# Two requests for key rows move from SyncE to ScalarE's queue, and steps of the engines are put in another order

## The chip, the cores and the metric

The kernel runs on one core of one Trainium2 chip. The metric is device time in microseconds, as the median of several executions; lower is better. The core has TensorE (PE in the profile), VectorE (DVE), ScalarE (ACT), GpSimd (POOL) and SyncE (SP), each with an instruction stream of its own that it works through in order, and 16 DMA engines that carry out transfers which an engine's instruction asks for.

## The reference

Attention in chunks of 64 tokens, then a feed-forward layer with a short convolution as its gate. Shapes: q, k, v are 8 x 8 x 576 x 64, so d_model = 512 and d_ff = 1024.

```
scores = scale * matmul(q_c, k_c.T)          # per head, chunk of 64
attn = exp(scores - max); attn = attn / (sum(attn) + 1e-09)
x = matmul(attn, v_c)  -> (batch, seq, heads * head_dim)
h = maximum(x @ w_in, 0)
conv_out = sum over k of conv_w[k] * shifted h
out = (h * sigmoid(conv_out)) @ w_out
```

The weights arrive as 64-bit floats and are turned into pairs of 32-bit ones on the chip.

## The kernel before, in words

The work is cut into 36 attention tiles of 128 tokens (two chunks each), and into 12 units of 384 tokens for the first product of the feed-forward layer (x @ w_in, line 411, called MM1 here). The second product (line 515) takes tokens by pairs of tiles. x and the weights are kept as a high and a low part (x_h and x_l, wi_h and wi_l), so that each product takes three passes.

For an early tile, rows of q and k are loaded into one of three buffers (`load_rows`, line 129; the buffers are named qk with a number), transposed on TensorE (line 198) in two halves, and each half is copied out of PSUM into qkT by ScalarE or VectorE (lines 77 and 79). Then come the scores (line 250), the maximum, the subtraction, the exponential, the sum and the scaling (lines 260 to 282 and 322), a transposition of the result (line 329), the product with v (line 342), and x_h and x_l (lines 397 and 401). The weights are loaded into two buffers (line 547; w_in in six pieces, conv_w, then w_out) and split by lines 561, 565, 570, 77 or 79, and 574. MM1 of the first unit needs tiles 0 to 2.

Nothing is scheduled while the kernel runs. A list `steps` holds every step. A table `moved_` says which steps go to another engine than their usual one, a table `order_` gives the order in which a planner places them, and the planner's begin times give the order in which each engine gets its instructions. Loads and stores are all issued by SyncE, in order, and the issue of a load waits until its buffer is free. Each transfer signals one of eight semaphores in turn, so an issue also waits until the transfer eight places before it has landed.

Two pieces of code are written out around the steps. The constants: `ident_r`, a copy of the identity that ScalarE makes, and `rebias`. And filler matmuls (line 1161), products of `ident_r` with itself whose result nobody reads. They are put on TensorE where the planner sees a gap, up to its planned time 110, and the first group stands at the very start. Their number follows from the length of the gap.

Of the kernel before, what the change touches and what calls it, by code (L numbers as in the profile page):

```python
# [23 lines left out]
AF = mybir.ActivationFunctionType  # L24
# [6 lines left out]
def attn_ffn(ctx: ExitStack, tc: tile.TileContext, q, k, v, w_in, conv_w, w_out, out):  # L31
    nc = tc.nc
# [5 lines left out]
    NCK = S // C  # L38
# [33 lines left out]
    steps = []  # L72
# [20 lines left out]
    ident = const.tile([P, P], F32, name="ident")  # L93
    make_identity(nc, ident)
    ident_r = const.tile([P, P], F32R, name="ident_r")
    nc.scalar.copy(out=ident_r, in_=ident)
    rebias = const.tile([P, 1], F32, name="rebias")
    nc.scalar.activation(out=rebias, in_=ident[:, 0:1], func=AF.Exp)
    nc.gpsimd.memset(rebias, -896.0 * 2 ** 23)
# [23 lines left out]
    def load_rows(st, t):  # L123
        if t < NP:
            r = row_slot(st).rearrange("(p two) (h c) -> two p h c", two=2, h=H)
            (b0, t0), (b1, t1) = chunk(2 * t), chunk(2 * t + 1)
            for i, src in enumerate((q, k)):
                for b, t_, p0, n in [(b0, t0, 0, C)] if b0 == b1 else [(b0, t0, 0, C // 2), (b1, t1, C // 2, C // 2)]:
                    nc.sync.dma_start(out=r[i, p0:p0 + n], in_=src[b, :, t_:t_ + 2 * n, :].rearrange("h (p e) d -> p h (e d)", e=2))  # L129
            return  # L130
        r = row_slot(st).rearrange("p (i c) -> p i c", i=2)
        (b0, t0), (b1, t1) = chunk(2 * t), chunk(2 * t + 1)
        for i, src in enumerate((q, k)):
            rows = r[:, i].rearrange("p (h d) -> p h d", d=D)
            for b, t_, p0, n in [(b0, t0, 0, P)] if b0 == b1 else [(b0, t0, 0, C), (b1, t1, C, C)]:
                nc.sync.dma_start(out=rows[p0:p0 + n], in_=src[b, :, t_:t_ + n, :].rearrange("h i d -> i h d"))
# [557 lines left out]
    def att(t, key, load_key, writes):  # L694

        st = {"t": t}
        if t < NAT:
            r = "slot"
            ld = step("SP", 1.25 if (2 * t) % NCK < NCK - 1 else 2.5, load_key, load_rows, (st, t), take=[(r, st)],
# [259 lines left out]
    for s, over in x_writes:  # L959
# [21 lines left out]
    ]  # L981
    for i, n in (divmod(x, 4) for x in moved_):
# [171 lines left out]
    for i in sorted(order_, key=lambda i: begin[i]):  # L1154
# [11 lines left out]
        steps[i]["fn"](*steps[i]["args"], *([steps[i]["eng"]] if steps[i]["other"] else []))  # L1166
        if steps[i]["port"]:
            made[i] = list(nc.cur_bb.bb.instructions)[n:]
# [40 lines left out]
```

## Time and profile before

| | us |
|---|---|
| median of 3 executions | 469.8 (469.11 to 470.95) |
| the profiled execution, its own time | 470.28 |
| its span, first to last instruction | 468.5 |
| PE busy in the span | 456.2 (97%) |
| DVE busy | 409.6 (87%) |
| ACT busy | 263.7 (56%) |
| POOL busy | 283.5 (61%) |

Matmuls are pipelined and overlap in the records, so a busy PE is an engine that always has something under way. The profiled execution took 1.78 us more than its span, and 0.48 us more than the median.

### The profile page before, as it was taken

To read this page: it belongs to the slowest core of one execution; us is meant where nothing else is said; L and a number is where in the kernel's file an instruction comes from. 1 tells how busy PE (TensorE), PEld (TensorE's weight loads), DVE (VectorE), ACT (ScalarE), POOL (GpSimd) and SP (SyncE) were. 2 spreads that over 40 slices of the span, in tenths; PEclk is the share of its full clock that TensorE was granted. 3 is DMA by queue.
4 is the path that set the end of the run, shared out by engine and by line. 5 is a ranking of instruction groups with operands and counts; after the bars stand their busy time and mean duration, and the time that the engine had idled before them with its cause. 6 is when DMAs were issued, how large, how long until landed. Compare 5 with 4: busy or idle time off the path is not lost.

```text
span 468.5 us, 13076 instructions
## 1 busy us (share of the span) xinstructions
PE 456.2 (97%) x5287; PEld 444.3 (95%) x5287; DVE 409.6 (87%) x771; ACT 263.7 (56%) x544; POOL 283.5 (61%) x256
## 2 busy tenths in 40 slices
PE   7899899999999999999999999999999999999996
PEld 7779798999999999999999999999999999999996
DVE  2899999999999899989788889998989987977784
ACT  3589988756646555564444564455556453542641
POOL 0344768847686654979678967755856643448221
PEclk9999999999999999999999999999999999999999
DMA  7999999999896839687987495741215101100012
GB/s 223 248 305 306 246 149 218 158 177 209 147 158 175 191 95 178 126 158 180 181 182 182 109 172 111 169 128 33 58 35 157 25 24 29 40 17 31 22 46 91
DMA packets 184320, 64.32 MB, mean 137 GB/s; under 512 B 155564, under 2 KB 175044, under 8 KB 184260
## 3 DMA queue, kind: packets, MB, share of 16 engines
q1 hardware_dynamic: 184260, 63.48, 62.7%
q8 instruction: 42, 0.69, 0.6%
q14 instruction: 18, 0.15, 0.1%
HBM read 50.88 MB, written 23.59 MB: 159 GB/s over the span
## 4 chain that ended last, share of the span: by engine, by line
PE 80%; DVE 9%; DMA 5%; ACT 2%; issue 1%; SPq 1%; POOL 1%; DVEq 0%; ACTq 0%; POOLq 0%
PE b_ps L411 36%; PE b_ps L515 36%; DVE gt L454 2%; PE sx_ps L250 2%; PE sx_ps L342 2%; PE z_ps L342 2%; DMA v<-in_v 1%; DMA w<-in_moe_w_out 1%; DVE f L502 1%; DMA qk<-in_k 1%; DMA w<-in_moe_conv_w 1%; DVE wt L570 1%; PE z_ps L250 1%; PE b_ps L329 1%; SPq L129 1%
## 5 line engine op out<-in xcount | busy, mean ns | idle before, releaser
L515 PE MATMUL b_ps<-wo_h,f 128*128 128x256 f32 x1008 | 190.9, 282 | 0.4 <-DVE wt L533 0.3
L515 PEld LDWEIGHTS b_ps<-wo_h,f 128*128 128x128 f32 x1008 | 158.8, 188 | 2.0 <-issue 0.5
L515 PE MATMUL b_ps<-wo_l,f 128*128 128x256 f32 x504 | 141.2, 280 | 0.0
L454 DVE SCALAR_TENSOR_TENSOR gt<-b_ps,cw,gt 128x384 f32<-128x384 f32 (+3 forms) x208 | 116.4, 576 | 11.2 <-ACT gt L449 9.1
L502 POOL TENSOR_TENSOR f<-gt,f 128x512 fp32r<-128x512 f32 x67 | 86.4, 1294 | 45.5 <-ACT f L77 16.3
L515 PEld LDWEIGHTS b_ps<-wo_l,f 128*128 128x128 f32 x504 | 94.9, 188 | 0.0
L411 PE MATMUL b_ps<-x_h,wi_h 128*128 128x386 f32 (+2 forms) x384 | 84.6, 342 | 0.0
L411 PE MATMUL b_ps<-x_l,wi_h 128*128 128x386 f32 (+2 forms) x384 | 83.3, 339 | 0.0
L411 PE MATMUL b_ps<-x_h,wi_l 128*128 128x386 f32 (+2 forms) x384 | 83.1, 338 | 0.0
L465 ACT ACTIVATE gt<-gt 128x384 f32<-128x384 f32 (+2 forms) x96 | 49.9, 524 | 54.5 <-DVE gt L454 54.2
L411 PEld LDWEIGHTS b_ps<-x_l,wi_h 128*128 128x128 f32 x384 | 68.8, 188 | 0.0
L411 PEld LDWEIGHTS b_ps<-x_h,wi_l 128*128 128x128 f32 x384 | 68.6, 188 | 0.0
L449 ACT ACTIVATE gt<-b_ps,cw 128x384 f32<-128x384 f32 (+2 forms) x104 | 56.5, 556 | 20.6 <-DVE b_ps L421 18.5
L411 PEld LDWEIGHTS b_ps<-x_h,wi_h 128*128 128x128 f32 x384 | 65.5, 188 | 1.0 <-ACT gt L449 0.2
L505 POOL TENSOR_TENSOR gt<-gt 128x512 f32<-128x512 f32 x41 | 52.8, 1295 | 15.3 <-DVE gb L505 6.0
L484 DVE SCALAR_TENSOR_TENSOR gt<-gt,b_ps 128x192 f32<-128x192 f32 (+2 forms) x120 | 47.2, 410 | 8.8 <-ACT gt L465 8.5
L419 ACT ACTIVATE b_ps<-b_ps 128x386 f32<-128x386 f32 (+2 forms) x79 | 37.6, 479 | 28.2 <-PE b_ps L411 27.0
L79 POOL CAST f<-gt 128x512 fp32r<-128x512 f32 x43 | 26.9, 625 | 21.2 <-PE b_ps L515 18.0
L527 ACT ACTIVATE wt<-b_ps 128x256 f32<-128x256 f32 x54 | 20.6, 381 | 29.8 <-PE b_ps L515 29.7
L77 ACT CAST f<-gt 128x512 fp32r<-128x512 f32 x44 | 26.9, 617 | 14.8 <-PE b_ps L515 8.5
L502 POOL TENSOR_TENSOR f<-gb,f 128x512 fp32r<-128x512 f32 x18 | 23.2, 1294 | 17.9 <-DVE f L502 9.9
L220 DVE STREAM_TRANSPOSE qkT<-qk 128x1024 f32<-128x1024 f32 (+1 forms) x30 | 33.4, 1121 | 0.0
(99 smaller groups left out, 585.6 us busy)
## 6 DMA issues: line engine op xcount, KB each, us to landing
out<-wt SPq DMA_DIRECT2D x36, 256.0 KB, 2.7
qk<-rows SPq DMA_DIRECT2D x24, 320.0 KB, 5.8
rows<-in_q SPq DMA_DIRECT2D x12, 576.0 KB, 8.1
rows<-in_k SPq DMA_DIRECT2D x12, 576.0 KB, 7.8
qk<-rows SPq DMA_DIRECT2D x24, 256.0 KB, 4.6
v<-in_v SPq DMA_DIRECT2D x21, 256.0 KB, 5.0
w<-in_moe_w_out SPq DMA_DIRECT2D x4, 1024.0 KB, 6.5
wt<-wt SPq DMA_DIRECT2D x48, 64.0 KB, 2.0
```

The costliest lines, as they stand in the source:

```text
L77: nc.scalar.copy(out=out, in_=in_)
L79: ENG[eng].tensor_copy(out=out, in_=in_)
L220: nc.vector.transpose(out=to[:, :, i:i + n], in_=of[:, :, o:o + n])
L411: nc.tensor.matmul(h_ps[:, 0:w], lhsT=wt[:, f // 2, kt, P * (f % 2):P * (f % 2) + P], rhs=xt[:, u % NX, kt, 0:w], start=n == 0, stop=n == ...
L419: nc.scalar.activation(out=h, in_=h, func=AF.Relu)
L449: nc.scalar.mul(out=g, in_=h, mul=cw[:, FT + f:FT + f + 1])
L454: nc.vector.scalar_tensor_tensor(out=g, in0=h, scalar=w, in1=g, op0=ALU.mult, op1=ALU.add)
L465: nc.scalar.activation(out=g, in_=g, func=AF.Tanh, scale=0.5)
L484: nc.vector.scalar_tensor_tensor(out=o, in0=g, scalar=1.0, in1=hv, op0=ALU.add, op1=ALU.mult)
L502: ENG[eng].tensor_tensor(out=part(st, 1), in0=quarter(*src), in1=part(st, 0).bitcast(F32), op=ALU.subtract)
L505: ENG[eng].tensor_tensor(out=quarter(*out_), in0=quarter(*a), in1=quarter(*b), op=op)
L515: nc.tensor.matmul(o, lhsT=part(ft, a)[:, j, :], rhs=w[:, i, j, :], start=first and n == 0, stop=n == 3 * FT // 2 - 1, skip_group_check=True)
```

## The change

Three things. ScalarE instead of SyncE issues the k rows of tiles 0 and 1. The instructions that make the constants are written behind the loads of tile 1, so that on ScalarE they stand behind the two issues. And the tables `moved_` and `order_` are new up to planned times near 100 us; behind that they are as before. The planner is told that SyncE is held 0.65 instead of 1.25 for a load of tiles 0 and 1.

```
-    nc.scalar.copy(out=ident_r, in_=ident)
     rebias = const.tile([P, 1], F32, name="rebias")
-    nc.scalar.activation(out=rebias, in_=ident[:, 0:1], func=AF.Exp)
-    nc.gpsimd.memset(rebias, -896.0 * 2 ** 23)
+
+    def constants():
+        nc.scalar.copy(out=ident_r, in_=ident)
+        nc.scalar.activation(out=rebias, in_=ident[:, 0:1], func=AF.Exp)
+        nc.gpsimd.memset(rebias, -896.0 * 2 ** 23)
...
-                    nc.sync.dma_start(out=r[i, p0:p0 + n], in_=src[b, :, t_:t_ + 2 * n, :].rearrange("h (p e) d -> p h (e d)", e=2))
+                    (nc.scalar if i and t < 2 else nc.sync).dma_start(out=r[i, p0:p0 + n], in_=src[b, :, t_:t_ + 2 * n, :].rearrange("h (p e) d -> p h (e d)", e=2))
...
-            ld = step("SP", 1.25 if (2 * t) % NCK < NCK - 1 else 2.5, load_key, load_rows, (st, t), take=[(r, st)],
+            ld = step("SP", 0.65 if t < 2 else 1.25 if (2 * t) % NCK < NCK - 1 else 2.5, load_key, load_rows, (st, t), take=[(r, st)],
...
     moved_ = [
-        89, 113, 141, 165, 186, 225, 353, 505, 793, 801, 817, 969, 977, 1045, 1121, 1129, 1197, 1205, 1465,
+        65, 89, 93, 165, 186, 225, 353, 457, 465, 793, 801, 817, 933, 969, 1009, 1045, 1093, 1121, 1129, 1197,
...
     order_ = [
-        84, 85, 103, 87, 88, 0, 104, 18, 1, 86, 2, 105, 3, 90, 4, 5, 89, 91, 6, 122, 92, 19, 20, 7, 106, 107, 8,
+        84, 85, 87, 86, 103, 104, 18, 0, 1, 88, 105, 2, 4, 3, 90, 91, 19, 106, 107, 5, 6, 92, 109, 89, 93, 122,
...
         steps[i]["fn"](*steps[i]["args"], *([steps[i]["eng"]] if steps[i]["other"] else []))
+        if steps[i]["fn"] is load_rows and steps[i]["args"][1] == 1:
+            constants()
```

Line numbers of the changed kernel are 2 higher than before from the constants on, and 4 higher from line 1170 on. Its buffers have other numbers: qk_96, 97 and 98 are what qk_99, 100 and 101 were, w_99 and w_100 what w_102 and w_103 were.

The start of ScalarE's stream before (ident_r and rebias are the constants, b_ps a bank of PSUM):

```order
L96 ACT_TABLE_LOAD
L96 CAST ident_r<-ident 128x128
L98 ACTIVATE rebias<-ident 128x1
L77 COPY qkT<-b_ps 128x2x2x2x64 x2
L609 ACTIVATE wt<-wt,rebias 24x128
L561 ACTIVATE wt<-w_102 128x512
```

The same place now:

```order
L131 DMA qk_96<-in_k 64x8x128
L131 DMA qk_97<-in_k 64x8x128
L99 ACT_TABLE_LOAD
L99 CAST ident_r<-ident 128x128
L100 ACTIVATE rebias<-ident 128x1
L77 COPY qkT<-b_ps 128x2x2x2x64 x2
L611 ACTIVATE wt<-wt,rebias 24x128
L563 ACTIVATE wt<-w_99 128x512
```

The load of the activation table and the copy that makes ident_r now stand behind two DMA issues; SyncE's stream is the same as before without these two.

TensorE's stream keeps the order of its work; only fillers change in number and place. The first group has 10 instead of 12, the group ahead of the fourth tile's scores 10 instead of 6. Here is the place ahead of MM1's first matmul, before (qkT and p_all are the operands of scores and of the product with v):

```order
L250 MATMUL sx_ps<-qkT 64x64 x16
L1161 MATMUL b_ps<-ident_r 128x256 x2
L1161 MATMUL b_ps<-ident_r 128x512
L342 MATMUL sx_ps<-p_all,v 64x64 x16
L198 MATMUL b_ps<-ident,qk_99 64x128 x16
L411 MATMUL b_ps<-x_h,wi_h 128x384 x4
```

And now:

```order
L252 MATMUL sx_ps<-qkT 64x64 x16
L344 MATMUL sx_ps<-p_all,v 64x64 x16
L200 MATMUL b_ps<-ident,qk_96 64x128 x16
L413 MATMUL b_ps<-x_h,wi_h 128x384 x4
```

The three fillers are gone. Three others, of 128x512, which stood ahead of the second unit's MM1, now stand ahead of a product with v in the first unit's.

VectorE's stream from the maximum of tile 0 on, before (m is the maximum, z the sum, w_103 the buffer with conv_w, w_102 that with the first piece of w_in):

```order
L260 TENSOR_REDUCE m<-sx_ps 128x2x4
L622 SCALAR_TENSOR_TENSOR wt<-w_103,wt 24x128
L264 TENSOR_TENSOR wt<-sx_ps,m 128x2x4x64
L565 TENSOR_SCALAR wt<-wt 128x512
L630 TENSOR_SCALAR wt<-wt 24x128
L635 SCALAR_TENSOR_TENSOR wt<-wt 24x128
L570 SCALAR_TENSOR_TENSOR wt<-w_102,wt 128x512
L260 TENSOR_REDUCE m<-sx_ps 128x2x4
L264 TENSOR_TENSOR wt<-sx_ps,m 128x2x4x64
L273 TENSOR_REDUCE z<-wt 128x8
```

The same place now:

```order
L262 TENSOR_REDUCE m<-sx_ps 128x2x4
L619 SCALAR_TENSOR_TENSOR wt<-w_100,wt 24x128
L624 SCALAR_TENSOR_TENSOR wt<-w_100,wt 24x128
L266 TENSOR_TENSOR wt<-sx_ps,m 128x2x4x64
L632 TENSOR_SCALAR wt<-wt 24x128
L567 TENSOR_SCALAR wt<-wt 128x512
L572 SCALAR_TENSOR_TENSOR wt<-w_99,wt 128x512
L275 TENSOR_REDUCE z<-wt 128x8
L281 TENSOR_SCALAR z<-z 128x8
L284 RECIPROCAL z<-z 128x8
```

One step on conv_w now follows tile 0's maximum, and tile 0's sum comes ahead of tile 1's maximum. Up to x_l of tile 2 VectorE has two copies into qkT more than before (4 instead of 2; ScalarE has two fewer) and one addition on z fewer. Over the whole program VectorE further gains one copy into p_all and loses one rectification (line 421).

## Rows read from the trace of the kernel before

**Rows 1.** The page's first part: busy time, share of the span, instructions.
```profile
PE 456.2 (97%) x5287; PEld 444.3 (95%) x5287; DVE 409.6 (87%) x771; ACT 263.7 (56%) x544; POOL 283.5 (61%) x256
```

**Rows 2.** TensorE by stretch: us, busy (matmuls), granted clock, DMA share, GB/s.
```profile
35.00:80.00 45.00, 42.52 (x446) 1.00 1.04 230
80.00:460.00 380.00, 379.60 (x4250) 1.00 0.57 115
```

**Rows 3.** Chain that ended last, up to 35 us: start, us, what.
```profile
4.25 5.40 DMA w<-in_moe_conv_w
...
13.62 6.60 DMA v<-in_v
...
20.96 5.43 DMA qk<-in_k
...
26.44 1.13 PE b_ps L198 x16
...
31.06 0.67 PE b_ps L1161 x3
```

**Rows 4.** All engines, 10.27 to 34.43 us: busy PE, PEld, DVE, ACT, POOL; clock; DMA share.
```profile
10.27:34.43 24.16, 21.40 (x463) 17.96 (x460) 21.61 (x46) 16.70 (x32) 8.90 (x11) 1.00 0.97 281
```

**Rows 5.** Timeline, first 11 us: start, us, engine, instruction, idle time ahead and releaser.
```profile
0.73 1.28 ACT L96 ACT_TABLE_LOAD   x1 [0.73 <-PEq L1194]
...
1.55 0.63 SPq L129 DMA_DIRECT2D qk<-in_k  x1
2.02 0.30 ACT L96 CAST ident_r<-ident 128x128 fp32r<-128x128 f32 x1
...
2.37 2.93 PE L1161 MATMUL b_ps<-ident_r 128*128 128x256 f32 x12 [2.37 <-ACT ident_r L96]
...
5.24 4.07 PE L198 MATMUL b_ps<-ident,qk 128*64 128x128 f32 x48
...
8.44 1.01 SPq L129 DMA_DIRECT2D qk<-in_q  x1
8.45 0.69 DVE L79 COPY qkT<-b_ps 128x512 f32<-128x512 f32 x1 [8.45 <-PE b_ps L198]
...
10.27 0.67 DVE L260 TENSOR_REDUCE m<-sx_ps 128x8 f32<-128x512 f32 x1
```

**Rows 6.** DMA issue between 1.5 and 2.0 us: KB, us to landing.
```profile
qk<-in_k SPq DMA_DIRECT2D x1, 256.0 KB, 3.6
```

**Rows 7.** TensorE alone, two stretches in tile 0's and 1's transpositions; columns as in Rows 2.
```profile
5.50:7.50 2.00, 2.00 (x22) 1.00 0.79 241
8.00:8.75 0.75, 0.75 (x18) 1.00 1.10 323
```

**Rows 8.** All engines, two early stretches; the last two numbers: DMA share, GB/s.
```profile
2.25:3.00 0.75, 0.63 (x3) 0.63 (x4) 0.00 (x0) 0.17 (x2) 0.10 (x1) 1.00 0.51 137
...
6.00:7.25 1.25, 1.25 (x16) 1.25 (x14) 0.00 (x0) 0.00 (x0) 0.00 (x0) 1.00 0.65 216
```

**Rows 9.** Timeline of TensorE at MM1's start, and of VectorE's x_l for tile 2.
```profile
34.26 0.97 PE L411 MATMUL b_ps<-x_h,wi_h 128*128 128x384 f32 x4
35.06 0.86 PE L411 MATMUL b_ps<-x_l,wi_h 128*128 128x384 f32 x4
...
33.67 0.76 DVE L401 TENSOR_TENSOR x_l<-sx_ps,x_h 128x512 fp32r<-128x512 f32 x2
```

**Rows 10.** TensorE's waits from 34 us to the end: us, times, longest.
```profile
PE sx_ps L342 <- ACT gt L465: 1.0, 1, 1.0
PE b_ps L329 <- ACT b_ps L419: 1.0, 1, 1.0
```

**Rows 11.** VectorE by line up to 34 us: count, busy, mean ns, idle ahead and releaser.
```profile
L565 DVE TENSOR_SCALAR wt<-wt 128x512 uint32<-128x512 uint32 (+1 forms) x5 | 2.7, 543 | 1.1 <-ACT wt L561 1.1
...
L79 DVE COPY qkT<-b_ps 128x512 f32<-128x512 f32 x2 | 1.3, 667 | 8.4 <-PE b_ps L198 8.4
L279 DVE TENSOR_SCALAR z<-z 128x8 f32<-128x8 f32 x3 | 0.5, 168 | 0.1
```

94 rows, old and new, of tables (moved_, order_) are left out of this document.

## The prediction

> **What bounds the kernel now.** I read the page's first part, then TensorE's busy time by stretch, then its waits, then the chain that ended last, from the left. TensorE is busy for 97% of the span [rows 1], and where it is not lies early: of the 45 us from 35 to 80 it is idle for 45 - 42.52 = 2.48, of the 380 behind that for 0.40 [rows 2]. Two waits of 1.0 us make up most of the 2.48, for ScalarE's steps behind MM1 [rows 10]. So from MM1's first matmul at 34.26 [rows 9] the rest is a train of matmuls with 2.9 us of holes. The end comes earlier by as much as MM1 starts earlier, and by holes that close; it can hardly come earlier otherwise, as the change takes no matmul out of that train.
>
> What sets MM1's start? The chain up to there is made of transfers and the issues between them: conv_w lands at 4.25 + 5.40 = 9.65, a v transfer issued at 13.62 lands at 20.22, and the k rows of tile 5, issued at 20.96, land at 26.39 [rows 3]. From 26.44 on TensorE has no gap worth naming up to MM1: transpositions, scores, three fillers of 0.67 us together, and so on [rows 3, 9]. Meanwhile the DMA engines are busy for 97% of 10.27 to 34.43, and VectorE for 21.61 of these 24.16 us, which leaves it 2.55 idle [rows 4]. VectorE ends x_l of tile 2 at 33.67 + 0.76 = 34.43; its first reader is MM1's fifth matmul at 35.06 [rows 9], so that VectorE may be 0.6 later there before TensorE waits. Three paths are thus close to one another: transfers, TensorE's order, VectorE's work.
>
> **The change part by part.** *Transfers.* SyncE loses two issues of 0.63 each [rows 5], so that what follows them on SyncE, the first piece of w_in, conv_w and the first v, is asked for some 1.3 us earlier, and k of tile 0 stands in a queue at 0.73 instead of 1.55. Whether that is 1.3 us for the bytes is another matter. From 2.25 to 3.00 the DMA engines are at 0.51 and from 6.00 to 7.25 at 0.65 [rows 8]; full use of both stretches would give 0.75 x 0.49 + 1.25 x 0.35 = 0.81 us, and at 97% from 10 us on there is little else to fill. Bounds: 0 (the first stretch is start-up, the second has another cause than late issues) to 0.81. I take 0.4 at the landing of tile 5's k, half, as the first stretch is what a second request at 0.73 should fill best.
>
> The Trainium skill speaks against more: its page "DMA: Bandwidth & Descriptors", section "Issuing engines are not separate DMA queues", says that requests of several engines end on the same 16 DMA engines and that one saves only the time of asking. By that rule this term would be 0 and the sum 0.4 us higher; a share below 1 in the two stretches is what the trace has against it.
>
> *ScalarE's first work.* The table load (1.28) and the copy of ident_r (0.30) begin at 0.73 and the first filler starts at 2.37 [rows 5]. Now two issues stand ahead. No row shows an issue on ScalarE; the nearest are SyncE's, 0.63 each [rows 5]. Bounds: nothing, if ScalarE hands a request over at once, to 1.4 us for both with the gaps between; I take 1.4, by the nearest row. Then the fillers start near 3.8. Twelve of them lasted from 2.37 to 5.24, 0.24 each [rows 5], so ten end near 6.2. Before, tile 0's k landed at 1.55 + 3.6 = 5.15 [rows 6] and the transpositions began at 5.24 at once; now they stand behind fillers on an engine that works in order, and begin about 0.95 late although their data are there earlier. What the earlier k could give is lost here.
>
> How fast they then run is unsure. In 5.50 to 7.50 there are 22 matmuls in 2.00 us, in 8.00 to 8.75 there are 18 in 0.75, of the same kind [rows 7]. The granted clock's column says 1.00 in both, but by the rate TensorE ran at the lower of its two levels, 1.2 GHz, until shortly before 8 us, after it had been idle to 2.37 and busy without a gap since [rows 5]. A start 1.4 us later may put the rise 1.4 us later, or leave it. So tile 0's maximum on VectorE, at 10.27 [rows 5], comes between 0 and 1.4 later; I take 0.7, the middle: the work until then on half rate costs more, conv_w's share of VectorE's work comes earlier.
>
> *What waits behind it.* SyncE's load for tile 3 takes the buffer of tile 0, and it was issued at 8.44, when TensorE had just left it (VectorE's copy of the last half starts at 8.45) [rows 5]. It moves with the transpositions, to 9 or 9.5, and in order behind it on SyncE stand k of tile 3, the second and third pieces of w_in and the v transfer of the chain. At 97% busy DMA engines the queue has work in hand, v takes 6.60 us from issue to landing [rows 3]; this is why I let it eat only the part of the 0.8 above that I have not taken.
>
> *VectorE's steps.* Two more copies into qkT at 0.67 and one addition fewer at 0.17 [rows 11]; consecutive steps overlap by some 0.06, so +1.13 up to x_l of tile 2. With 0.7 of lateness this is 1.83 us, against 2.55 of idle time [rows 4] and 0.6 of room ahead of MM1's fifth matmul. The idle time is mostly waits for ScalarE [rows 11], which loses those two copies, but also for pieces of w_in, so not all of it can be used. If all of it is used and the room too, nothing is passed on; if none is used, 1.83 - 0.6 = 1.2, and with the upper bound of lateness 1.9. I take 0.45. The other re-ordered steps up to 100 us have the same work and durations; I cost them at 0, covered by the 2.48 of holes [rows 2], and their uncertainty goes into the last rival. On ScalarE and VectorE what changes hands later (one copy into p_all, one rectification) cancels to a few tenths where TensorE has no holes.
>
> *Fillers.* Three of 0.67 us stand in the gapless stretch ahead of MM1 [rows 3] and go: -0.67; bounds 0, if another path then sets the start, to -0.67. The four more ahead of tile 3's scores (0.24 each at most [rows 5]) fall where TensorE waits for VectorE's and ScalarE's steps; in 10.27 to 34.43 it is idle for 24.16 - 21.40 = 2.76 [rows 4]. The three of 128x512 only change place, ahead of work that waits: 0.
>
> *The sum*, against the profiled execution's 470.28: -0.40 (transfers) - 0.67 (fillers) + 0.45 (lateness that is passed on) = -0.62, so 469.7. That execution is 0.48 above the median of the three, 469.8, which gives **469.2** for a median.
>
> **The rivals.** *One: the late ident_r passes through, slower.* ScalarE's two issues delay the fillers, these the transpositions of tile 0, these the release of its buffer, and SyncE's whole queue moves with it. For this: the copy at 8.45 and the issue at 8.44 [rows 5] hang on one event, and k of tile 5 is on the chain [rows 3]. Against: a queue with 6.60 us from issue to landing. If its landing moves by the full 1.4 and the fillers give 0.67 back, +0.7; if VectorE's 1.13 come on top unabsorbed, +1.9: 470.5 to 471.7 as a median. It decides against the change once the lateness passed on exceeds 0.67 + 0.4 = 1.07. A further hole behind MM1 takes it past 472.
>
> *Two: nothing is gained.* q and k of two tiles share the DMA engines, a tile's transpositions need both, and the same bytes stand in line as before. Transfers 0, fillers -0.67, lateness +0.45 to +0.7: 469.6 to 469.8. For it: DMA engines that are 97% busy [rows 4]; against it: the two stretches that are not [rows 8]. It is what the page's rule, cited above, comes to.
>
> *Three: the new order closes holes, clearly faster.* If the 2.48 us between 35 and 80 close by half to all [rows 2, 10], with MM1 0.6 to 1.1 earlier: -1.8 to -3.6, so 466.2 to 468.0. For it: both long waits are single events of order, not of load. Against it: VectorE and ScalarE, whose steps TensorE waits for there, get no less work.
>
> **How the numbers follow.** The likeliest case 0.45, rival one 0.22, rival two 0.18, rival three 0.15. Three reruns of the kernel before spread over 1.84 us, so about 0.5%, 2.35 us, is what a measurement can tell from no change. Faster by more than that means below 467.45: rival three's greater part and some of what I have not thought of, 0.14. Slower means above 472.15: the upper end of rival one, 0.12. Within: 0.74. The range leaves out the outer part of rival three and the end of rival one: 467.2 to 471.8. The likeliest case alone has 468.2 to 470.4: 469.2 with the bounds of its terms (-0.4 and -0.2 for transfers and lateness better than taken, +1.2 for fillers and lateness worse) and the spread between medians.
>
> **What would show it.** Right: ScalarE's table load starts near 2.2 and the first filler near 3.8; the first transposition starts near 6.2, not earlier than before; the DMA share from 2.25 to 3.00 rises; tile 5's k lands near 26.0; MM1 starts near 33.6; from there TensorE has about 2.9 us of holes. Wrong: a first filler before 3 us (ScalarE's issues are cheap, and the sum falls by what I passed on), MM1 at 35 or later (rival one), or MM1 near 33.6 with holes of under 1.5 or over 4 us behind it, where the new order and not the start decides.

## The result, and the profile after

The changed kernel takes 473.05 us, median of nine runs, against 470.24 for the kernel before on the same chip: ratio 1.0052, 95% interval 1.0031 to 1.0072. By the ratio that is 2.4 us slower; the two medians lie 2.8 apart. The profiled execution of the changed kernel took 471.16 us, the least of its nine, span 469.4, and so lies only 0.9 above that of before; the section below shows why one trace against one trace says too little. Ratios here and below compare executions at a granted clock of 0.99 or more; one of run f1 below, the profiled one, ran at 0.85 and is left out.

Engine totals and TensorE by stretch, after, beside [rows 1, 2]:

```profile
PE 455.1 (97%) x5286; PEld 443.3 (94%) x5286; DVE 411.6 (88%) x772; ACT 262.3 (56%) x543; POOL 283.5 (60%) x256
```

```profile
35.00:80.00 45.00, 42.29 (x445) 1.00 1.02 228
80.00:460.00 380.00, 378.38 (x4235) 1.00 0.57 115
```

Holes behind the start are 2.71 + 1.62 = 4.33 us, before 2.88. The start, timeline of the changed kernel, beside [rows 5]:

```profile
0.73 1.41 ACTq L131 DMA_DIRECT2D qk<-in_k  x2
...
0.73 1.67 SPq L131 DMA_DIRECT2D qk<-in_q  x2
...
2.17 1.28 ACT L99 ACT_TABLE_LOAD   x1 [2.17 <-issue]
2.44 0.63 SPq L549 DMA_DIRECT2D w<-in_moe_w_in  x1
...
3.81 2.50 PE L1163 MATMUL b_ps<-ident_r 128*128 128x256 f32 x10 [3.81 <-ACT ident_r L99]
...
33.68 0.96 PE L413 MATMUL b_ps<-x_h,wi_h 128*128 128x384 f32 x4
```

ScalarE's two issues take 1.41 us, its table load, the copy of ident_r and TensorE's first filler come 1.44 later, and MM1 starts at 33.68, before at 34.26 [rows 9]. TensorE's waits from 34 to 120 us, after, beside [rows 10] (line, releaser, us in total, times, longest):

```profile
PE b_ps L413 <- ACT qkT L77: 1.1, 1, 1.1
PE sx_ps L344 <- ACT p_all L77: 1.0, 1, 1.0
PE b_ps L331 <- DVE gb L486: 0.7, 1, 0.7
PE sx_ps L344 <- DVE x_l L403: 0.4, 1, 0.4
PE b_ps L517 <- DVE gt L486: 0.3, 1, 0.3
```

One of the two long waits of before is gone (that of L329 for ScalarE's rectification), one, at 58.6 us, has only another name, and four are new: 0.4 near 52 us, 1.1 at 61.4, 0.3 at 83, 0.7 at 113. Two short ones of before that [rows 10] does not show (0.20 at 54.85 for VectorE's gb, 0.25 at 56.98 for ScalarE's x_h) are gone too. Now the stretch from the first MM1 to unit 1's first, of before and then of after, each with the stretch from 10 us to that MM1 ahead of it (columns as in [rows 4]):

```profile
10.00:34.26 24.26, 21.50 (x465) 18.06 (x464) 21.68 (x45) 16.92 (x31) 8.73 (x11) 1.00 0.96 281
34.26:60.94 26.68, 25.18 (x321) 23.30 (x320) 26.41 (x50) 25.09 (x50) 15.68 (x14) 1.00 1.01 259
```

```profile
10.00:33.68 23.68, 21.09 (x481) 18.12 (x471) 22.29 (x45) 15.23 (x29) 8.58 (x11) 1.00 0.92 278
33.68:61.44 27.76, 25.17 (x322) 23.25 (x320) 26.74 (x51) 26.66 (x53) 15.57 (x14) 1.00 1.01 256
```

TensorE does the same 25.2 us in both. VectorE, third, is busy for 26.41 of 26.68 us before, ScalarE, fourth, for 25.09. In the changed kernel ScalarE does 1.69 less ahead of MM1 and 1.57 more behind it, and the stretch is 1.08 longer. VectorE does 0.33 more in it and has 1.02 idle there, where it had 0.27. By instruction counts, two more of ScalarE's copies stand behind MM1 (one into p_all, one into qkT), and one more conversion L563 (1.15), with one cast of 128x1024 into wo_h less and two of 128x256 more.

What makes unit 1's MM1 late is seen on ScalarE's timeline, after:

```profile
57.65 0.59 ACT L77 COPY p_all<-b_ps 128x512 f32<-128x512 f32 x1 [0.27 <-PE b_ps L331]
58.13 1.18 ACT L563 ACTIVATE wt<-w 128x1024 f32<-128x1024 f32 x1
59.19 0.58 ACT L451 ACTIVATE gt<-b_ps,cw 128x383 f32<-128x383 f32 x1
59.84 0.65 ACT L399 CAST x_h<-sx_ps 128x4 fp32r<-128x4 f32 x2
60.38 0.54 ACT L467 ACTIVATE gt<-gt 128x383 f32<-128x383 f32 x1
60.80 0.59 ACT L77 COPY qkT<-b_ps 128x512 f32<-128x512 f32 x1
```

There is no gap over 0.1 us in it: the copy at 60.80 gives back the bank that MM1 waits for, and behind the p_all copy four other steps come first, of which the conversion is the longest. Before, that conversion began only at 62.67.

The second new loss, VectorE's timeline of the changed kernel:

```profile
106.56 0.68 DVE L79 COPY p_all<-b_ps 128x512 f32<-128x512 f32 x1
107.16 1.59 DVE L504 TENSOR_TENSOR f<-gb,f 128x512 fp32r<-128x512 f32 x1
...
110.86 1.24 DVE L222 STREAM_TRANSPOSE qkT<-qk 128x1024 f32<-128x1024 f32 x1
112.02 0.38 DVE L531 TENSOR_SCALAR wt<-b_ps 128x256 f32<-128x256 f32 x1
112.33 0.40 DVE L486 SCALAR_TENSOR_TENSOR gt<-gt,b_ps 128x256 f32<-128x256 f32 x1
112.66 0.27 DVE L486 SCALAR_TENSOR_TENSOR gb<-gt,b_ps 128x128 f32<-128x128 f32 x1
```

L486 gives back the bank for the transposition of P, and TensorE waits for it until 112.98. The copy stands on VectorE only in the new order; a factor's step like L504 stands there before too, at 105.60, and took 0.69.

**Where the difference of the two traces lies.** MM1 has 96 blocks of twelve matmuls, eight for each unit. From the starts of their first matmuls: MM1 -0.58; first block to unit 1's first +1.08; unit 1's first to unit 2's first +0.03; unit 2's first, the 17th of the 96, to the 21st, below "17 to 21", +0.88 (21.19 before, 22.07 after); from there to TensorE's last matmul +0.25; from that (ends at 464.19 and 465.85) to the span's end -0.79. Sum +0.87.

### The profile page after: what moved, and what is told of

It reads as the page before. It is cut to its first block, busy times and chain, and to the rows that moved or that the text cites. A ratio compares the mean times of both kernels' runs of the same rounds, so it can differ in the third digit from the quotient of the medians.

```text
span 469.4 us, 13061 instructions
## 1 busy us (share of the span) xinstructions
PE 455.1 (97%) x5286; PEld 443.3 (94%) x5286; DVE 411.6 (88%) x772; ACT 262.3 (56%) x543; POOL 283.5 (60%) x256
## 4 chain that ended last, share of the span: by engine, by line
PE 75%; DVE 16%; ACT 4%; issue 2%; DMA 1%; ACTq 0%; DVEq 0%
PE b_ps L413 36%; PE b_ps L517 32%; DVE gt L456 3%; DVE f L504 2%; PE z_ps L344 2%; PE sx_ps L344 2%; PE sx_ps L252 1%; DMA w<-in_moe_w_in 1%; DVE z L275 1%; DVE wt L572 1%; DVE m L262 1%; DVE wt L266 1%; PE z_ps L252 1%; DVE gt L486 1%; DVE qkT L222 1%
## 5 line engine op out<-in xcount | busy, mean ns | idle before, releaser
L504 POOL TENSOR_TENSOR f<-gt,f 128x512 fp32r<-128x512 f32 x68 | 87.7, 1294 | 47.6 <-ACT f L77 17.8
L486 DVE SCALAR_TENSOR_TENSOR gt<-gt,b_ps 128x192 f32<-128x192 f32 (+2 forms) x120 | 47.2, 411 | 8.8 <-ACT gt L467 8.5
L504 POOL TENSOR_TENSOR f<-gb,f 128x512 fp32r<-128x512 f32 x17 | 21.9, 1294 | 15.6 <-DVE f L504 7.7
```

The source lines that it names most:

```text
L486: nc.vector.scalar_tensor_tensor(out=o, in0=g, scalar=1.0, in1=hv, op0=ALU.add, op1=ALU.mult)
L504: ENG[eng].tensor_tensor(out=part(st, 1), in0=quarter(*src), in1=part(st, 0).bitcast(F32), op=ALU.subtract)
```

## The experiments

order_ is taken in three pieces: I, its first 172 steps, planned up to about 36 us; II, steps 173 to 385, to about 85 us; III, steps 386 to 499, to about 115 us. The sets of steps in each are the same in both kernels, and behind III the tables are equal. Steps change engines in I and III only. "Unit 0" is the time from the first MM1 to unit 1's first, "17 to 21" as above. All ratios are to the kernel before on the same chip; the last three columns are of one trace each.

| kernel | k issued by | I | II | III | ratio (95%) | first MM1 | unit 0 | 17 to 21 |
|---|---|---|---|---|---|---|---|---|
| before | SyncE | old | old | old | 1 | 34.26 | 26.68 | 21.19 |
| after | ScalarE | new | new | new | 1.0052 (1.0031 to 1.0072) | 33.68 | 27.76 | 22.07 |
| e1_sync_issue | SyncE | new | new | new | 1.0058 (1.0039 to 1.0077) | 33.68 | 27.95 | 22.04 |
| e2_issue_only | ScalarE | old | old | old | 1.0006 (0.9988 to 1.0024) | 35.25 | 26.63 | 21.19 |
| e3_early_order | ScalarE | new | old | old | 1.0011 (0.9993 to 1.0029) | 34.75 | 27.39 | 21.19 |
| e8_early_sync | SyncE | new | old | old | 1.0011 (0.9991 to 1.0031) | 35.14 | 27.43 | 21.19 |
| e4_late_order | SyncE | old | new | new | 1.0045 (1.0026 to 1.0065) | 34.03 | 27.19 | 22.05 |
| e5_middle_order | SyncE | old | new | old | 1.0017 (0.9998 to 1.0037) | 34.88 | 27.07 | 21.20 |
| e6_last_order | SyncE | old | old | new | 1.0002 (0.9983 to 1.0022) | 35.65 | 26.33 | 21.68 |

The edits, against the changed kernel for e1 and the kernel before for e2:

```diff
+    constants()
...
-                    (nc.scalar if i and t < 2 else nc.sync).dma_start(out=r[i, p0:p0 + n], ...
+                    nc.sync.dma_start(out=r[i, p0:p0 + n], ...
...
-        if steps[i]["fn"] is load_rows and steps[i]["args"][1] == 1:
-            constants()
```

```diff
-    nc.scalar.copy(out=ident_r, in_=ident)
...
+    def constants():
+        nc.scalar.copy(out=ident_r, in_=ident)
...
-                    nc.sync.dma_start(out=r[i, p0:p0 + n], ...
+                    (nc.scalar if i and t < 2 else nc.sync).dma_start(out=r[i, p0:p0 + n], ...
...
+        if steps[i]["fn"] is load_rows and steps[i]["args"][1] == 1:
+            constants()
```

> The changed kernel's order of steps on every engine, but SyncE issues the k rows of tiles 0 and 1 again and the constants are made first, as before. Theory A (the loss is in the new order of steps behind the first MM1): the first transposition is back near 5.2 us, the first MM1 starts between 33.7 and 34.4, and the kernel is still slower than before by 2 to 4 us (ratio 1.004 to 1.008). Theory B (the loss comes from ScalarE's two DMA issues and the late ident_r, the prediction's first rival): without them the loss is gone, ratio 0.998 to 1.002.

> The kernel before with its own order of steps; only the two k issues go to ScalarE and the constants are made behind them, with 12 first fillers. Theory A: the first fillers start near 3.8 us and the first transposition near 6.5, the first MM1 stays within 0.5 us of 34.26, and the time within 1 us of before (ratio 0.998 to 1.002). Theory B: slower by 2 to 3 us, ratio 1.004 to 1.006.

In the others whole pieces of the table change hands; where pieces I and II meet, e4 and e5 differ from before by

```diff
-        ..., 78, 79, 282, 295, 48, 255, 145, 183, ...
+        ..., 78, 79, 48, 282, 183, 295, 158, 159, ...
```

> The changed kernel up to the first MM1 matmuls (its issue by ScalarE and its order of the first 172 steps, planned up to about 36 us), and behind them the order and the engines of the kernel before; the three 128x512 fillers stand where they stood before. Theory A: the first MM1 starts near 33.7 as in the changed kernel and the gain is kept or partly kept, ratio 0.9975 to 1.000 (469 to 470.2 us). Theory B: ratio 1.003 to 1.006, as the changed kernel.

> The kernel before up to the first MM1 matmuls (SyncE issues all rows, its own order of the first 172 steps), and behind them the order and the engines of the changed kernel. Theory A: the first MM1 starts near 34.3 as before, and the holes of the changed kernel at 61, 77 and 83 us are there, ratio 1.005 to 1.008 (+2.4 to +3.6 us). Theory B: no loss, ratio 0.998 to 1.002.

> The kernel before with one stretch of its order replaced by the changed kernel's: the 213 steps planned between about 36 and 85 us (same engines, another order, and the three 128x512 fillers ahead of a product of unit 0 instead of ahead of unit 1's MM1). Theory A1 (the loss is made in this stretch: TensorE waits near 52 us for x_l and near 61 us for a bank that ScalarE's qkT copy gives back): both waits are there, ratio 1.002 to 1.005. Theory A2 (the loss is made behind 85 us, where steps change engines): ratio 0.999 to 1.001, and the wait for b_ps near 78 us of the kernel before stays.

> The kernel before with the changed kernel's last new stretch alone: the steps planned between about 85 and 115 us, with the steps that change engines there (unit 2's rectification and two factors' steps, the softmax sums and the p_all copy of tiles 9 and 10). Theory A1: ratio 0.999 to 1.001. Theory A2: ratio 1.003 to 1.005, with a wait of TensorE for gb near 113 us (0.65 in the changed kernel) that the kernel before does not have.

> The new order of the first 172 steps with SyncE issuing all rows, and behind them the order of the kernel before: the late order and ScalarE's issue are both left out. If the parts add up, the first MM1 starts at or before 33.7 us as in the kernel with the whole new order and SyncE's issue, and the time is that of before or up to 0.6 us less (ratio 0.9985 to 1.0005). If the new early order itself costs, ratio 1.002 or more.

Theory A held against B: without ScalarE's issues the loss stays (e1), with them alone there is none to be seen (e2). What e3 was to keep of the early MM1 it did not: its MM1 started at 34.75 and unit 0 took 27.39; e8's started at 35.14, where 33.7 or less was expected. e4 has the changed kernel's waits at 61 and 83 us and none near 77, where the changed kernel has none either; its ratio lies a little below the range. In the traces pieces I and II each lengthen unit 0, by 0.9 to 1.0 (e3, e8) and 0.6 to 0.7 (e4, e5) against a mean of 26.47 with both old, and III lengthens 17 to 21 by 0.5 alone and by 0.86 with II ahead of it. That A1 alone or A2 alone would account for the loss was wrong: both of A1's waits are in e5, but its ratio is below A1's range, and e6 has A2's wait for gb (0.42) at a ratio of 1.0002. By the traces all three pieces add to the loss; in the times no piece alone stands clear of 1.

**The changed kernel once more**, e7_after_again, no edit:

> The changed kernel once more, for a second trace: its first shows a span of 469.4 us, less than the median of its runs. If the loss of the median is made in the stretches that the first trace shows, the waits of TensorE at 52, 58.6, 61.4, 83 and 113 us are there again and the longer span comes with longer waits there; if something else adds to it, the extra time stands elsewhere, in the start or behind 130 us.

472.53 us, span 470.7: MM1 at 34.73, unit 0 27.38, 17 to 21 22.05. Four of the five waits are there again within 0.02, the small one near 52 us is not. The span is 1.4 longer by the start (+1.05) and the tail (+0.71), while first MM1 to last matmul is 0.39 shorter. In the twenty traces of this study the first MM1 starts anywhere from 33.48 to 36.12, and from 33.48 to 35.65 with one and the same order of the start. So the first trace's -0.58 is no gain that the change made: on the mean MM1 starts at 34.51 in the seven traces with SyncE's issue and old piece I, and at 34.90 in nine with ScalarE's issue and new piece I (f1's left out). What repeats is the inside: unit 0 takes 26.23 to 26.68 us (mean 26.47, four traces) with old pieces I and II and 27.38 to 28.21 (mean 27.90, six traces) with new ones; the difference of 1.43 with the 0.86 of 17 to 21 makes 2.3 us, against 2.4 measured. Unit 0 is not longer only because MM1 starts earlier: in e2 and e6 MM1 starts at 35.25 and 35.65 and unit 0 takes 26.63 and 26.33, in e7 it starts at 34.73 and unit 0 takes 27.38. What goes with the length is ScalarE's busy time in it: 24.98 to 25.14 us with I and II old, 25.77 to 25.92 with one of them new (unit 0 27.07 to 27.43), 26.59 to 26.67 with both new.

**Taking single waits away.** f2 puts one qkT copy ahead of the conversion and no filler ahead of unit 1's MM1; f1 puts steps near 110 us in another order; f3 does both; f4 is f2 with the old piece III.

```diff
-        302, 287, 303, 293, 58, ..., 188, 450, 71,
+        302, 287, 303, 450, 293, 58, ..., 188, 71,
...
-        if steps[i]["eng"] == "PE" and begin[i] <= until_:
+        if steps[i]["eng"] == "PE" and begin[i] <= until_ and i != 328:
```

```diff
-        472, 496, 497, 516, 517, 607, 612, 387, 388, 576, 514, 515, 608, 615,
+        472, 514, 496, 497, 516, 517, 607, 608, 515, 387, 388, 612, 576, 615,
```

> The changed kernel with some steps of unit 2's blocks put in another order near 110 us: on ScalarE the sigmoid L467 of the second block directly behind that of the first, ahead of two rectifications and a convolution; on VectorE the reciprocal and the products L486 behind that sigmoid and the copy L531, all ahead of tile 12's transposition (1.24 us). Theory A (the waits that the new order makes are the loss): TensorE's wait for gb near 113 us (0.65) is gone, and the time from the first MM1 to the end of the span falls from 435.7 to 436.0 to about 435.2, ratio to before 1.002 to 1.005. Theory C (VectorE and ScalarE are full and a wait that is taken away comes back further on): the wait is gone there, another of about its size stands behind it, the stretch stays 435.7 to 436.0, ratio 1.004 to 1.007.

> The changed kernel with one copy moved on ScalarE: tile 8's first qkT copy, which stands at 62.96 us, goes directly behind the p_all copy at 57.65, ahead of the 1.18 us conversion step L563; no filler is placed ahead of unit 1's first MM1. Theory A: TensorE's wait of 1.07 ahead of unit 1's MM1 at 61.44 is gone, that MM1 starts 26.6 to 27.0 us behind the first one instead of 27.4 to 27.8, and the stretch from the first MM1 to the end falls to about 434.7 to 435.0, ratio 1.001 to 1.004. Theory C: the MM1 starts earlier, but later waits for VectorE's products take up the gain, ratio 1.004 to 1.007.

> Both of these edits in the changed kernel. Theory A: both waits are gone and the stretch from the first MM1 to the end is 434.0 to 434.4, as in the kernel before (434.24) or shorter, since its wait of 0.99 at 77.8 us does not stand in the new order either; ratio 0.998 to 1.002. Theory C: ratio 1.003 to 1.007.

> The changed kernel with the copy moved as in the second edit, and behind 85 us (planned) the order and the engines of the kernel before. Theory A: the waits at 61.4 and 113 us are gone and that at 77.8 us too; the stretch from the first MM1 to the end is 433.3 to 434.2, ratio 0.997 to 1.001. Theory C: ratio 1.001 to 1.004.

Ratios: f1 1.0077 (1.0060 to 1.0093), f2 1.0054 (1.0033 to 1.0075), f3 1.0062 (1.0038 to 1.0087), f4 1.0056 (1.0036 to 1.0075). f1's trace is left out here. TensorE's waits from 34 to 120 us in f2:

```profile
PE sx_ps L344 <- ACT p_all L77: 1.0, 1, 1.0
PE b_ps L331 <- POOL wt L324: 0.7, 1, 0.7
PE b_ps L331 <- DVE gb L486: 0.7, 1, 0.7
PE sx_ps L344 <- DVE x_l L403: 0.6, 1, 0.6
PE b_ps L517 <- DVE gt L486: 0.3, 1, 0.3
```

The wait of 1.07 is gone, unit 0 takes 27.16 (f3: 26.80), and unit 1 in its place 36.0 instead of 35.4: a wait of 0.7 for P's normalization on GpSimd, at 79 us, is new. Theory C held for f2 and f3: a wait taken away came back further on, though mostly for GpSimd and not for the two engines that C names, and none of the four is faster than the changed kernel. The ratios of f1 and f4 lie above C's ranges (1.004 to 1.007, 1.001 to 1.004). In f3 17 to 21 fell to 21.67, in f4, with old piece III, to 21.19. f4 also shows a wait of 1.32 at 41.8, for GpSimd again, in a stretch whose order is that of the changed kernel; that one stays unexplained, and with it unit 0 takes 28.39, which takes up what the old piece III gives back.

**Doses.** To the kernel before, time is added on one engine by an instruction that is done twice and leaves the same values: in unit 0 a conversion on ScalarE (g1) or a step on VectorE (g3), and as control two convolutions on ScalarE near 210 us (g2).

```diff
+        if i == 49:
+            steps[i]["args"][0]["times"] = 2
...
+        for _ in range(st.get("times", 1)):
             nc.scalar.activation(out=st["T"], in_=st["H"].bitcast(F32), func=AF.Prelu, ...
```

g3 has step 51 and L570 in the same form; g2:

```diff
+            for _ in range(2 if u == 5 and f in (1, 2) else 1):
                 nc.scalar.mul(out=g, in_=h, mul=cw[:, FT + f:FT + f + 1])
```

> The kernel before, with one conversion on ScalarE (L561, 128x1024, about 1.15 us) done twice in unit 0's stretch, near 47 to 50 us; the second writes the same values again. Theory D (unit 0's stretch, from the first MM1 to unit 1's, is bound by ScalarE, 25.09 of its 26.68 us busy, and VectorE, 26.41 busy, not by TensorE): the stretch grows from 26.3 to 26.7 us by 0.6 to 1.2, and most of it is still there at the end, ratio to before 1.001 to 1.003. Theory E (TensorE bounds it and ScalarE has slack): the stretch stays 26.3 to 26.7, ratio 0.999 to 1.001.

> The control: the kernel before, with the same amount of ScalarE's time added where ScalarE is about half busy, in unit 5 (two convolutions L449 of 0.57 us each done twice, near 210 us). Both theories: nothing, ratio 0.999 to 1.001, and the time from the first MM1 to unit 1's stays 26.3 to 26.7.

> The kernel before, with one step of VectorE (L570, 128x1024, 1.22 us) done twice in unit 0's stretch, near 49 us; the second leaves the same values. Theory D: unit 0's stretch grows by 0.6 to 1.3 us, ratio 1.001 to 1.003. Theory E: nothing, ratio 0.999 to 1.001.

The unit 0 stretch of g1, g3 and g2 in this order, all engines, columns as above:

```profile
33.48:61.50 28.02, 25.22 (x321) 23.28 (x320) 26.47 (x50) 25.99 (x51) 15.67 (x14) 1.00 1.01 252
```

```profile
35.00:63.21 28.21, 25.24 (x322) 23.28 (x321) 27.61 (x51) 25.23 (x50) 15.62 (x14) 1.00 0.97 249
```

```profile
34.24:60.47 26.23, 24.94 (x321) 23.30 (x320) 26.23 (x49) 24.99 (x50) 15.47 (x14) 1.00 1.05 267
```

1.15 us more on ScalarE lengthen unit 0 by 1.3 to 1.8 against the four traces of before's order, 1.24 more on VectorE by 1.5 to 2.0. Theory D held for both engines, with more than the 0.6 to 1.3 that it gave. The control's dose runs long behind unit 0 and has to be read where it stands, from unit 5's first MM1 to unit 6's, before and then g2:

```profile
204.66:239.51 34.85, 34.85 (x358) 34.53 (x357) 29.52 (x54) 17.48 (x38) 30.22 (x26) 1.00 0.89 175
```

```profile
205.00:239.84 34.84, 34.84 (x358) 34.52 (x357) 29.55 (x54) 18.53 (x40) 30.24 (x26) 1.00 0.88 167
```

ScalarE does 1.05 more there, and the stretch is as long as before. The end follows in the traces: from the first MM1 to TensorE's last matmul 431.47 and 431.64 us, against 429.93 of before and 430.62 of the control. The times say it with less force: g3 1.0032 (1.0018 to 1.0047) is clear of 1, g1 1.0012 (0.9997 to 1.0028) neither of 1 nor of the control, g2 1.0007 (0.9990 to 1.0024). g3 also shows that a longer unit 0 does not by itself draw more of ScalarE's work into it: it takes 28.21 with ScalarE busy for 25.23.

**The second loss.** The changed kernel with one engine put back: g4 the rectification on VectorE, h1 the p_all copy on ScalarE, h2 that copy and L504 on GpSimd.

```diff
-        1837, 2094,
+        1837, 1985, 2094,
```

```diff
-        2285, 2301, 2353,
+        2285, 2353,
```

h2 also takes 1513 out.

> The changed kernel with one step put back to its engine of before: the rectification of a block of unit 2 near 108 us is on VectorE (L423) instead of ScalarE (L421), where it stands behind an exponential that ScalarE waits 2.55 us to start. If that move makes the loss of 0.88 us between 96 and 118 us, the wait for gb at 113 us is gone or under 0.2, that stretch (MM1 block 17 to block 21 of 96) falls from 22.05 us to 21.2 to 21.5, and the ratio to 1.003 to 1.004. If VectorE's new work there makes it (the copy into p_all and a factor's step that cost 0.68 and 1.59), the stretch stays at 21.9 or more, ratio 1.0045 to 1.0065.

> The changed kernel with one step put back to its engine of before: the copy of tile 9's P into p_all (0.68 us on VectorE at 106.56) is on ScalarE again, which waits for VectorE from 106.8 to 109.4 us there. If VectorE's added work makes the loss between 96 and 118 us, TensorE's wait for gb at 113 us (0.65) is gone and the stretch from MM1 block 17 to block 21 falls from 22.05 us to 21.2 to 21.6; ratio to before 1.002 to 1.005. If the wait comes from elsewhere, the stretch stays 21.9 to 22.1, ratio 1.0045 to 1.0065.

> The same, and also the factor's step L504 of 1.59 us at 107.16 back from VectorE to GpSimd, idle before 106.9. By the same reasoning VectorE is 2.3 us less busy there: the stretch from MM1 block 17 to block 21 is 21.2 to 21.3 as in the kernel before, unless GpSimd's longer step (1.29) makes a product wait; ratio 1.002 to 1.004. The loss ahead of unit 1's first MM1 (27.4 to 27.95 us instead of 26.3 to 26.7) stays in both.

17 to 21 took 22.41 us in g4, 21.67 in h1 (between the two ranges expected), 22.33 in h2 (not the 21.2 to 21.3 expected); the ratios are 1.0082 (1.0058 to 1.0105), 1.0057 (1.0035 to 1.0080) and 1.0080 (1.0062 to 1.0097). In the traces more work on VectorE there costs, less gives back, but only 0.4 of the 0.88, and in h1's ratio nothing of it shows. Nor is the 0.4 the price of the copy alone: L504 behind it, 1.59 in the changed kernel, takes 0.68 in h1. VectorE's timeline in h1 shows why it is not more:

```profile
108.05 0.68 DVE L504 TENSOR_TENSOR f<-gb,f 128x512 fp32r<-128x512 f32 x1
...
113.10 0.42 DVE L531 TENSOR_SCALAR wt<-b_ps 128x256 f32<-128x256 f32 x1 [0.79 <-PE b_ps L517]
113.44 0.41 DVE L486 SCALAR_TENSOR_TENSOR gt<-gt,b_ps 128x256 f32<-128x256 f32 x1
```

VectorE is now early, but L486 stands behind L531, which waits 0.79 for a product; TensorE still waits 0.42 for gb, 0.65 without h1's edit. h2 adds a wait of 0.39 for GpSimd's longer step. h1 together with f1's order was not tried.

## Why the prediction was wrong, step by step

- **The start** went as described and not as summed. Table load at 2.17 (forecast near 2.2), first filler 3.81 (3.8), first transposition 6.25 (6.2), SyncE's first w_in at 2.44 instead of 3.59, 1.15 earlier (1.3). The DMA share from 2.25 to 3.00, which was to rise, fell from 0.51 to 0.34, but it has 0.34 in e6 too, where SyncE issues all rows in the old order, and 0.66 in e3: the sign decides nothing. Tile 5's k landed at 25.42 (forecast near 26.0, before 26.39), and at 25.42 to 26.81 in the ten traces with ScalarE's issue, at 24.38 to 27.13 in the nine with SyncE's. MM1 at 33.68 against "near 33.6" is no confirmation: with SyncE's issue it is at 33.68 too (e1), and the same kernel had it at 34.73 (e7). The terms for transfers (-0.40) and lateness (+0.45) are below what these traces resolve. Of the lateness, tile 0's maximum starts at 10.27 in both traces of the pair and on the mean 0.65 later with ScalarE's issue (ten traces) than with SyncE's (nine), near the 0.7 that was taken; VectorE's two copies, less the addition, make 1.11 with the overlaps, not 1.13. e2, with the issue and the late ident_r but not VectorE's copies, gave 1.0006.
- **Rivals one and two.** The late ident_r did not make the loss (e1 has the loss without it). That the issue by ScalarE gains nothing agrees with e2 (to 0.2%, and e3 and e8, with and without it, both at 1.0011) and with the rule that the prediction cited from the Trainium skill, "DMA: Bandwidth & Descriptors", section "Issuing engines are not separate DMA queues".
- **Fillers**, -0.67: not found. The three are gone, and in the trace two waits of 0.55 and 0.50 (for P's normalization, and for VectorE's subtraction) stand between 28 and 31 us instead. The three 128x512 fillers in their new place were not tried by themselves.
- **The step that failed** is "the end comes earlier by as much as MM1 starts earlier", with "the other re-ordered steps up to 100 us ... I cost them at 0, covered by the 2.48 of holes". I took TensorE's train for the bound because TensorE is at 97% of the span. In unit 0 it is not: the row of that stretch, which I did not read, has VectorE at 26.41 and ScalarE at 25.09 of 26.68, and added time on either lengthens it (g1, g3). The holes of TensorE were not room for the new order but the trace of two other engines that were nearly full. With the new order ScalarE has 1.57 us more behind MM1, and unit 0 is longer by 1.1 in this pair and by 1.4 on the means. That this work is what lengthens it is argued from the doses and from ScalarE's busy time by pieces; the moved steps were not put back one by one. Nor did MM1 start 0.6 earlier, on the means above.
- **The cover at 96 to 118 us.** "what changes hands later (one copy into p_all, one rectification) cancels to a few tenths where TensorE has no holes": +0.86, of which the copy on VectorE, with the slow L504 behind it, makes 0.4; that the rest is the order in which L486 stands is argued from h1's trace and not shown.
- **The unknown was put on one side.** The uncertainty of the re-ordered steps went into rival three, as a gain. Its mirror, holes that open, was named at the end of rival one ("A further hole behind MM1 takes it past 472", on top of a late start) and in the last sentence (holes over 4 us behind MM1, "where the new order and not the start decides"); they are 4.33. Without a late start it had no price and no chance, and it is what happened. One part of rival three did happen: the wait at 77.8 closed.

## What to carry to other kernels

An engine at 97% of the span need not be the bound of the stretch in which its holes lie: read all engines' busy time from one event to the next there, and where another engine is nearly full (here VectorE 99%, ScalarE 94%), cost what a new order moves across that event at full length, to either sign. Against a single trace with a start that varies by 2 us, measure inside: the time between two events that both kernels have repeated to 0.5 us (unit 0, old order) and 0.8 (new). Taking away the wait that the profile names gained nothing here: another stood further on.

## What was not expected of the hardware

- The start varies from execution to execution more than the change under study. Tile 0's and tile 1's 48 transpositions took 3.33 us after and 4.24 in e3, whose start is the same, 4.07 before and 3.64 in e4, whose start is that of before, with the granted clock's column at 1.00 in all; from the last matmul to the span's end it took 3.5 to 4.6 us.
- The same 128x512 step on VectorE, L504, took 1.59 us at 107.16, while GpSimd's own L504 ran from 106.92 to 108.20, and 0.68 at 108.05 in h1, where GpSimd's began later, at 108.43. In the changed kernel's trace VectorE has 41 such steps of 128x512: the seven that begin while one of GpSimd's TENSOR_TENSOR steps runs take 0.88 to 1.59, the other 34 take 0.65 to 0.69. The Trainium skill, "GPSIMD Engine Reference", section "1. Specifications", says that GpSimd shares its SBUF interfaces with VectorE and that the two contend when a VectorE instruction has two SBUF inputs, as this one has; these durations agree with it.
- A dose of 1.15 us on ScalarE, busy for 94% of unit 0, cost 1.3 to 1.8, more than its length; why it is more was not tried.
